# Reordering the picking, the last loads and the last values of each layer in a four-layer decode kernel

## The chip, the cores and the metric

One core of a Trainium2 chip runs the whole program. The metric is the device time of one execution in microseconds (us), as the median of several runs. All runs quoted were in the same (fast) state: the executions of one kernel lie within 0.3% of their median. The span of a profile is the time from its first to its last instruction; over all runs it is 1.7 to 3.6 us shorter than the run's time.

In profiles, PE is the engine for matrix products (PEld its loading of weights), DVE the one for vectors, ACT the one for scalar functions, POOL a general one, and SP issues the loads (its queue is SPq). PSUM is the memory that takes PE's results. The granted clock is the share of its full clock that a throttle leaves PE. K9 is K of pair 9, and so on.

## The reference, cut to what matters

Four attention layers with one query token each; layers 0 and 2 use one set of weights and caches (A), layers 1 and 3 the other (B).

```python
# per layer; D = 640, 32 heads, 8192 keys, head size 192, all bf16
q = layernorm(x) @ wq                         # wq: 640 x 6144
p = softmax(q . k_cache * 192**-0.5)          # k_cache: 32 x 8192 x 192
o = p . v_cache                               # v_cache: 32 x 8192 x 192
x = x + o.reshape(6144) @ wo                  # wo: 6144 x 640
```

Every byte of K and V is used once per layer, so the program mostly streams 848 MB from memory.

## The kernel before

A *pair* is two heads; a layer has 16. Buffers live in a pool of 8 slots of 24 KB per partition; half a pair's K or V (3072 KB) fills one slot. All big loads leave one queue (SP) in the fixed order of a list `plan`. A load stands there until the slots it goes into are free, and every load behind it stands too. `KEPT` holds K of pair 0 from layer 0 to layer 2 and V of pairs 14 and 15 from layer 1 to layer 3, so layer 2 works with four slots.

```python
KEPT = {0: {("k", 0)}, 1: {("v", 14), ("v", 15)}}

# a step list gives the order on the engines; "plan" the order of loads (cut)
steps.append(("m", l, p, 0))              # q*K, first half: DVE product, PE sum
if late is not None:
    steps.append(("e", l, late))          # picking of the pair before
steps.append(("m", l, p, 1))              # q*K, second half
if p == NPAIR - 1:
    steps.append(("v", l, p - 1))
steps.append(("s", l, p))                 # softmax
...
if p == NPAIR - 1:
    steps += [("e", l, p - 1), ("wc", l, 2), ("v", l, p), ("e", l, p)]
...
both(("wo", l, 2), ("wol", l))            # wol: wo's rows of the last pair

def products(p, u):                       # "m": frees the K half when PE is done
    for c in range(4):
        DV.op(k3[.., part c] = kin[.., part c] * q_sb)     # 128 x 3072, in place
    for each group of R columns:
        PE.op(S += ident . k3[.., group])                  # 24 matmuls

def gather(p):                            # "e": the picking
    for i in range(VK):                   # VK = 8
        DV.op(acc (+)= O[:, i*DH:(i+1)*DH] * pick[:, i])   # reads PSUM
    PE.op(TB = half . acc); AC.op(orow = TB / sum)
```

`values` ("v") multiplies V by the probabilities with 8 keys per group, so its result in PSUM has 8 blocks per head of which the picking keeps the diagonal. `columns` ("wc") turns the row of outputs into columns for the product with wo.

## Time and profile before

| | before |
|---|---|
| time, median of the first 3 runs | 2018.94 us (2017.25 to 2019.47) |
| span of the profile | 2015.6 us |
| bytes read | 848.36 MB |
| rate in ten quiet stretches of 110 to 420 us | 430 to 434 GB/s |
| 848.36 MB at 432 GB/s | 1964 us |
| so time lost to less than full transfer | 2015.6 - 1963.8 = 51.8 us |

The first lines are from the profile's page of the kernel before: busy time by engine, then granted TensorE clock and memory rate in 40 slices of about 50 us, then the engines' shares of the chain that ended last (the work followed back from the last instruction, at each step to what released it).

```profile
span 2015.6 us, 13729 instructions
PE 1278.0 (63%) x8246; PEld 146.2 (7%) x3074; DVE 1210.3 (60%) x1395; ACT 139.5 (7%) x461; POOL 4.4 (0%) x22
...
PEclk9787787888688788788877877877787877778777
GB/s 418 429 432 418 427 437 410 436 436 424 436 430 436 414 433 427 402 428 436 428 311 435 427 430 434 428 381 432 433 421 429 435 427 433 436 427 434 434 432 295
DMA packets 25773, 849.24 MB, mean 421 GB/s; under 512 B 3056, under 2 KB 3056, under 8 KB 3696
...
DMA 56%; DVE 24%; PE 18%; ACT 1%; issue 1%; SPq 0%
```

No engine is full, and the rate is flat but for a few slices (311, 381, 402 and the last). The Trainium skill, "DMA: Bandwidth & Descriptors", Anatomy of one DMA, gives the moving part of a transfer as bytes over 436e9 per second, for DMAs that the GpSimd engine issues; the 432 GB/s of this trace, whose loads SP issues, agree within 1%. Only time in which the queue runs dry, and the tail after the last byte, can be saved. The windows view shows five such stretches; three smaller ones, near 174, 325 and 679 us, are not printed here. Its columns are: the stretch in us, its length, busy time and instructions of each engine, granted clock, DMA share, GB/s.

```profile
core 0: us, PE busy (x) PEld busy (x) DVE busy (x) ACT busy (x) POOL busy (x), PEclk, DMA share, GB/s
832.00:838.00 6.00, 3.75 (x28) 0.40 (x12) 1.28 (x4) 1.31 (x5) 0.00 (x0) 0.96 0.48 163
...
1022.00:1028.00 6.00, 3.64 (x79) 3.63 (x80) 2.13 (x6) 0.27 (x1) 0.00 (x0) 0.64 0.05 18
...
1044.00:1048.00 4.00, 4.00 (x22) 0.09 (x3) 2.27 (x3) 0.00 (x0) 0.00 (x0) 1.00 0.04 14
1352.00:1358.00 6.00, 6.00 (x23) 0.10 (x1) 5.49 (x4) 0.00 (x0) 0.00 (x0) 0.77 0.16 70
...
2003.00:2015.60 12.60, 5.65 (x118) 4.83 (x106) 3.57 (x10) 0.27 (x1) 0.00 (x0) 0.64 0.01 0
```

Why the queue was dry at 832 us, the timeline shows. First the SP queue of before (start, length, engine, line, operation; each line is the issue of a load), then DVE and PE at the same place.

```profile
809.38 0.33 SPq L369 DMA_DIRECT2D pool<-in_B_wo_dram  x1
834.88 0.33 SPq L356 DMA_DIRECT2D pool<-in_B_k_cache_dram  x1
...
1005.26 28.58 SPq L363 DMA_DIRECT2D pool<-in_A_wq_dram  x3
1048.06 0.34 SPq L356 DMA_DIRECT2D pool<-in_A_v_cache_dram  x1
...
1333.20 5.77 SPq L358 DMA_DIRECT2D pool<-in_A_k_cache_dram  x2
1357.40 0.80 SPq L358 DMA_DIRECT2D pool<-in_A_v_cache_dram  x2
```

```profile
814.21 6.77 DVE L530 TENSOR_TENSOR pool<-pool,q_sb 128x3072 bf16<-128x3072 bf16 x4 [8.71 <-DMA pool<-in_B_k_cache_dram]
...
821.21 0.42 DVE L616 TENSOR_SCALAR acc<-OY,small 128x192 f32<-128x192 f32 x1
821.67 3.13 DVE L617 SCALAR_TENSOR_TENSOR acc<-OY,small,acc 128x192 f32<-128x192 f32 x7
824.72 6.76 DVE L530 TENSOR_TENSOR pool<-pool,q_sb 128x3072 bf16<-128x3072 bf16 x4
```

```profile
826.92 7.88 PE L58 MATMUL S<-pool,ident 128*128 128x512 bf16 x23
```

K10 is issued at 834.88, 25 us after the load before it, because it goes into the slots of K9. K9 lands at 814.2, but its second half is multiplied only after the 3.7 us of picking, and PE is done with it at 834.8. From 1333.2 the two halves of K10 are issued in layer 2, the second by 1339, and then nothing for 18 us, until 1357.4: V10's first half waits for the slot of K10's first half, and the other half stands behind it.

### The profile page before, as it was taken

The numbers are of one execution on the slowest core, as the hardware profiler recorded it, in microseconds if no ns is written. First come the engines' busy times: TensorE is split into PE (matmuls) and PEld (weight loads), VectorE is DVE, ScalarE is ACT, GpSimd is POOL, SyncE is SP. The second block draws the span as 40 slices with busy tenths as digits, with TensorE's granted clock in tenths as the row PEclk, the third lists the DMA queues.
The fourth block names the chain that finished last, engine by engine and source line by source line (L and its number), as shares of the span: only waits on it lengthen the run. The fifth ranks groups of instructions, "written<-read, shape, count | busy, mean of one in ns | idle before, by whom it ended". The sixth has DMA issues, their size and how long they took to land.

```text
span 2015.6 us, 13729 instructions
## 1 busy us (share of the span) xinstructions
PE 1278.0 (63%) x8246; PEld 146.2 (7%) x3074; DVE 1210.3 (60%) x1395; ACT 139.5 (7%) x461; POOL 4.4 (0%) x22
## 2 busy tenths in 40 slices
PE   3566566566557656566765675675766766666666
PEld 0001001000100100100010010010001001001001
DVE  3566565577356657567744675664764764765765
ACT  0000000000000000000010000000000100000000
POOL 0000000000000000000000000000000000000000
PEclk9787787888688788788877877877787877778777
DMA  9999999999999999999979999999999999999996
GB/s 418 429 432 418 427 437 410 436 436 424 436 430 436 414 433 427 402 428 436 428 311 435 427 430 434 428 381 432 433 421 429 435 427 433 436 427 434 434 432 295
DMA packets 25773, 849.24 MB, mean 421 GB/s; under 512 B 3056, under 2 KB 3056, under 8 KB 3696
## 3 DMA queue, kind: packets, MB, share of 16 engines
q1 hardware_dynamic: 25568, 848.38, 98.0%
q8 instruction: 44, 0.72, 0.1%
q14 instruction: 17, 0.14, 0.0%
q10 hardware_dynamic: 144, 0.00, 0.0%
HBM read 848.36 MB, written 0.00 MB: 421 GB/s over the span
## 4 chain that ended last, share of the span: by engine, by line
DMA 56%; DVE 24%; PE 18%; ACT 1%; issue 1%; SPq 0%
DMA pool<-in_A_k_cache_dram 27%; DMA pool<-in_B_k_cache_dram 27%; DVE pool L530 17%; PE S L58 11%; DVE acc L617 4%; PE OY L58 3%; PE OY L590 2%; DMA pool<-in_B_wq_dram 1%; DMA pool<-in_A_v_cache_dram 1%; PE S L543 1%; ACT p_sb L567 1%; PE OY L501 1%; DVE s_sb L552 1%; DVE acc L616 1%; PE TB L628 0%
## 5 line engine op out<-in xcount | busy, mean ns | idle before, releaser
L530 DVE TENSOR_TENSOR pool<-pool,q_sb 128x3072 bf16<-128x3072 bf16 x512 | 864.3, 1753 | 547.1 <-DMA pool<-in_A_k_cache_dram 279.3
L58 PE MATMUL S<-pool,ident 128*128 128x512 bf16 x2944 | 825.9, 440 | 21.4 <-DVE pool L530 20.9
L543 PE MATMUL S<-pool,ident 128*128 128x512 bf16 x128 | 66.4, 518 | 367.7 <-DVE pool L530 367.5
L58 PE MATMUL OY<-pool,p_sb 128*16 128x512 bf16 x2048 | 202.2, 479 | 0.0
L617 DVE SCALAR_TENSOR_TENSOR acc<-OY,small,acc 128x192 f32<-128x192 f32 x448 | 187.2, 418 | 15.7
L590 PE MATMUL OY<-pool,p_sb 128*16 128x512 bf16 x1024 | 124.8, 475 | 101.5 <-ACT p_sb L567 63.3
L552 DVE TENSOR_REDUCE s_sb<-S 128x64 f32<-128x512 f32 x128 | 88.2, 689 | 78.0 <-PE S L58 78.0
L628 PE MATMUL TB<-acc,small 128*1 128x192 f32 x240 | 56.4, 363 | 120.2 <-DVE acc L617 120.2
L639 ACT ACTIVATE rows<-TB,small 1x192 bf16<-1x192 f32 x120 | 43.2, 405 | 1044.2 <-PE TB L628 1044.2
L567 ACT ACTIVATE p_sb<-s_sb,small 64x128 bf16<-64x128 f32 x128 | 55.7, 435 | 155.8 <-DVE small L561 155.0
L489 ACT ACTIVATE q_sb<-QM 128x192 bf16<-128x192 f32 x60 | 19.9, 331 | 529.3 <-PE QM L483 529.3
L612 DVE RECIPROCAL small<-TB 1x2 f32<-1x2 f32 x64 | 11.2, 175 | 72.5 <-PE TB L599 36.4
L628 PEld LDWEIGHTS TB<-acc,small 128*1 128x1 f32 x240 | 16.1, 86 | 479.9 <-DVE acc L617 467.7
L590 PEld LDWEIGHTS OY<-pool,p_sb 128*16 128x16 bf16 x1024 | 30.1, 104 | 269.1 <-issue 176.1
L543 PEld LDWEIGHTS S<-pool,ident 128*128 128x128 bf16 x128 | 12.9, 101 | 502.7 <-DVE pool L530 495.0
L557 PE MATMUL QM<-ident,m_bf 128*64 128x64 bf16 x128 | 14.1, 216 | 54.4 <-DVE m_bf L554 53.8
L501 PE MATMUL OY<-oT,pool 128*128 128x1 bf16 x900 | 38.1, 178 | 2.2 <-ACT oT L515 2.2
L501 PEld LDWEIGHTS OY<-oT,pool 128*128 128x128 bf16 x900 | 37.0, 131 | 2.9 <-ACT oT L515 2.9
L561 DVE TENSOR_REDUCE small<-QM 128x1 f32<-128x64 f32 x64 | 14.4, 224 | 34.2 <-PE QM L557 34.2
L483 PEld LDWEIGHTS QM<-rows,one_b 1*64 1x64 bf16 x120 | 6.2, 100 | 384.5 <-issue 377.7
L616 DVE TENSOR_SCALAR acc<-OY,small 128x192 f32<-128x192 f32 x64 | 26.7, 417 | 1.9
L567 ACT ACTIVATION_READ_ACCUMULATOR p_sb<-s_sb,small 64x1 f32 x128 | 23.3, 182 | 0.0
(59 smaller groups left out, 179.8 us busy)
## 6 DMA issues: line engine op xcount, KB each, us to landing
pool<-in_B_k_cache_dram SPq DMA_DIRECT2D x30, 6144.0 KB, 35.9
pool<-in_A_v_cache_dram SPq DMA_DIRECT2D x28, 6144.0 KB, 24.7
pool<-in_B_v_cache_dram SPq DMA_DIRECT2D x28, 6144.0 KB, 29.5
pool<-in_A_k_cache_dram SPq DMA_DIRECT2D x16, 6144.0 KB, 32.0
pool<-in_A_k_cache_dram SPq DMA_DIRECT2D x30, 3072.0 KB, 19.2
pool<-in_A_v_cache_dram SPq DMA_DIRECT2D x8, 3072.0 KB, 17.1
pool<-in_A_wo_dram SPq DMA_DIRECT2D x6, 2400.0 KB, 19.6
pool<-in_B_v_cache_dram SPq DMA_DIRECT2D x4, 3072.0 KB, 33.3
```

The lines of the kernel that those rows point to most:

```text
L58: return t.add_instruction(mybir.InstMatmult(name=t.bass.get_next_instruction_name(), engine=mybir.EngineType.PE, ins=[t.lower_ap(rhs), t. ...
L489: lambda a: a.activation(q_sb[i][:], QM[:, 0:DH], ACT.Copy), e, last["q"][i], bank=QMu)
L501: e = PE.op(lambda t, i=i, c=c, f=y_first[0], fin=end and i == k - 1: t.matmul(YB[:, c:c + 1], lhsT=t3[:, i, c:D:DC], rhs=o[:, i:i + 1], s ...
L530: e = DV.op(lambda v, d0=d0: v.tensor_tensor(k3[:, :, d0:d0 + QD], kin[:, :, d0:d0 + QD], q_sb[qi][:, d0:d0 + QD].unsqueeze(1).broadcast_t ...
L543: t.matmul(S[:, :], lhsT=ident[:], rhs=k3[:, :, d0:d0 + R], start=True, stop=fin) if d0 == 0 else
L552: lambda v, u=u: v.tensor_reduce(s[:, u * JU:(u + 1) * JU], SP_[u][:].rearrange("p (j r) -> p j r", r=R), AX.X, ALU.add), ev_S[p, u], last ...
L567: ev_p[p] = AC.op(lambda a, h=h, r=r: a.activation(p_sb[par][r, :, h], s[r, :], ACT.Exp, bias=negm[par][r, 0:1], accum_out=l_col[par][r, h ...
L590: t.matmul(o, lhsT=x, rhs=y, start=f, stop=fin) if c == 0 else
L616: v.tensor_scalar(acc[:], O[:, 0:DH], pick[:, 0:1], None, ALU.mult) if i == 0 else
L617: v.scalar_tensor_tensor(out=acc[:], in0=O[:, i * DH:(i + 1) * DH], scalar=pick[:, i:i + 1], in1=acc[:], op0=ALU.mult, op1=ALU.add)), e if ...
L628: e = PE.op(lambda t, h=h: t.matmul(TB[96:97, C_O + h * DH:C_O + (h + 1) * DH], lhsT=half[:, h:h + 1], rhs=acc[:], start=True, stop=True), ...
L639: last["TO"] = last["row_written"] = AC.op(lambda a, h=h: a.activation(orow[:, o0 + h * DH:o0 + (h + 1) * DH], TB[96:97, C_O + h * DH:C_O ...
```

## The change

It reorders. No byte and no product is dropped, except six of eight picks per layer end.

1. The picking of pair p-1 comes behind both products of pair p.
2. In a layer's last pair, V14's matmuls come between the two products of pair 15; the last part of wo is loaded before V15 and multiplied between (layers 1 and 3: also behind) V15's halves; the last pair takes 2 keys per group, so 2 picks instead of 8.
3. wol goes into the buffer of the q rows, which is free once "wc" is done. With that, wq of layers 2 and 3 can be split 2/2/1 rows instead of 1/2/2.
4. Layer 2's first loads: K1's first half, V0, K1's second half.
5. Where V is loaded in halves, the half whose slot is free earlier goes first (V10 of layer 2).

```diff
-                if late is not None:
-                    steps.append(("e", l, late))
-                    late = None
+                if p == NPAIR - 1:
+                    steps.append(("v", l, p - 1))
                 steps.append(("m", l, p, 1))
...
+                elif p > 0 and p % PAIRS_W > 0 or p > 2 * PAIRS_W:
+                    steps.append(("e", l, p - 1))
                 steps.append(("s", l, p))
...
+                        if l == 2 and p == 1:
+                            i = plan.index(("k", l, 1, 0))
+                            plan[i - 2:i + 1] = [("k", l, 1, 0)] + plan[i - 2:i]
...
-            both(("wo", l, 2), ("wol", l))
+            plan.insert(-2, ("wo", l, 2))
+            steps += [("wc", l, 2), ("v", l, p, 0), ("wo", l, 2), ("v", l, p, 1)]
+            if NB[l]:
+                both(("wob", l))
+            steps.append(("e", l, p))
+            both(("wol", l))
...
+                if n[2] < NPAIR - 1 and not whole(*n[:3]) and max(map(released, before[n])) > max(map(released, before[m])):
+                    plan[i:i + 2] = [m, n]
+                    turn[n[1:3]] = (1, 0)
...
-    Q_PARTS = [[(0, 2), (2, 2), (4, 1)] if l < 2 else [(0, 1), (1, 2), (3, 2)] for l in range(NL)]
+    Q_PARTS = [(0, 2), (2, 2), (4, 1)]
...
-                    wol_rows(l), w["wo"][r0:r0 + PD].rearrange("(p i) n -> p (i n)", p=P)),
+                    rows[:], w["wo"][r0:r0 + PD].rearrange("(p i) n -> p (i n)", p=P)),
...
+                k = 2 if p == NPAIR - 1 else VK
...
-                for i in range(VK):
+                for i in range(2 if end else VK):
```

More of the change, by code (lines that the diff above doesn't have):

```diff
@@ L87, in build @@
     QW = H * DH
-    Q_PARTS = [[(0, 2), (2, 2), (4, 1)] if l < 2 else [(0, 1), (1, 2), (3, 2)] for l in range(NL)]
+    Q_PARTS = [(0, 2), (2, 2), (4, 1)]
     OI = PD // P
-    NB = 3
+    NB = [0, 5, 0, 5]
     G = 4
@@ L238, in build @@
                     steps.append(("wq", l, 1))
-                if late is not None:
-                    steps.append(("e", l, late))
-                    late = None
+                if p == NPAIR - 1:
+                    steps.append(("v", l, p - 1))
                 steps.append(("m", l, p, 1))
@@ L245, in build @@
                 if p == NPAIR - 1:
-                    steps.append(("v", l, p - 1))
+                    steps.append(("e", l, p - 1))
+                elif p > 0 and p % PAIRS_W > 0 or p > 2 * PAIRS_W:
+                    steps.append(("e", l, p - 1))
                 steps.append(("s", l, p))
@@ L249, in build @@
                     both(("wq", l, 1), ("wq", l, 2))
-                if p == NPAIR - 2:
-                    continue
-                vs_ = [p] if p < NPAIR - 1 else [p - 1, p]
-                for i in vs_:
-                    if first_load("v", l, i) == (l, i):
-                        plan += [("v", l, i, u) for u in range(2)]
-                if p == NPAIR - 1:
-                    steps += [("e", l, p - 1), ("wc", l, 2), ("v", l, p), ("e", l, p)]
-                else:
+                if p < NPAIR - 2:
+                    if first_load("v", l, p) == (l, p):
+                        plan += [("v", l, p, u) for u in range(2)]
+                        if l == 2 and p == 1:
+                            i = plan.index(("k", l, 1, 0))
+                            plan[i - 2:i + 1] = [("k", l, 1, 0)] + plan[i - 2:i]
                     steps.append(("v", l, p))
@@ L263, in build @@
                         both(("wo", l, b))
-                    else:
-                        late = p
-            both(("wo", l, 2), ("wol", l))
-        plan.append(("wob", NL - 1))
+            for i in (p - 1, p):
+                if first_load("v", l, i) == (l, i):
+                    plan += [("v", l, i, u) for u in range(2)]
+            plan.insert(-2, ("wo", l, 2))
[4 more added lines that the diff above has]
+            both(("wol", l))
         at = {n: i for i, n in enumerate(steps)}
@@ L275, in released @@
                     l, p = l + 2, ORDER[l + 2]["pairs"].index(pair(l, p))
-                return at[("v", l, p) if n[0] == "v" else ("m", l, p, n[3])]
-            return at[n]
+                return at[("v", l, p, 1) if n[0] == "v" and p == NPAIR - 1 else ("v", l, p) if n[0] == "v" else ("m", l, p, n[3])]
+            return at[("wob", n[1]) if n[0] == "wo" and n[2] == 2 and NB[n[1]] else n]
         place, before, holder = {}, {}, [None] * NSLOT
@@ L284, in allot @@
                 ns = [("wq", n[1], g) for g in range(3)]
-            elif n[0] == "v" or n[0] == "k" and whole(*n[:3]):
+            elif n[0] == "v" and (n[2] < NPAIR - 1 or n[1] == 1) or n[0] == "k" and whole(*n[:3]):
                 ns = [n[:3] + (u,) for u in range(2)]
@@ L301, in build @@
         for n in plan:
-            if n[0] == "wol" and n[1] + 1 < NL:
-                m = ("wq", n[1] + 1, 0)
-                allot(m)
-                before[n] = before[("wq", n[1] + 1, 2)] if n[1] == 0 else before[m]
+            if n[0] == "wol":
+                before[n] = [("wc", n[1], 2)]
             elif n[0] == "wob":
@@ L309, in build @@
                 allot(n)
+        turn = {}
+        for i, n in list(enumerate(plan)):
+            if n[0] == "v" and n[3] == 0:
+                m = n[:3] + (1,)
+                turn[n[1:3]] = (0, 1)
+                if n[2] < NPAIR - 1 and not whole(*n[:3]) and max(map(released, before[n])) > max(map(released, before[m])):
+                    plan[i:i + 2] = [m, n]
+                    turn[n[1:3]] = (1, 0)
         freed, landed = {}, {}
@@ L314, in wq_rows @@
         def wq_rows(l, g):
-            c0, k = Q_PARTS[l][g]
+            c0, k = Q_PARTS[g]
             if l < 2:
@@ L320, in wq_rows @@
             return slot[place[("wq", l, g)]][:, 0:k * QC].rearrange("p (c n) -> p c n", c=k)
-        def wol_rows(l):
-            if l + 1 == NL:
-                i = place[("wol", l)] * TS
-            else:
-                i = place[("wq", l + 1, 0)] * TS + (DC * QW if l == 0 else QC)
-            return pool[:, i:i + OI * D]
         def transfer(n):
@@ L344, in transfer @@
                 return SP.op(lambda s: s.dma_start(
-                    slot[place[("wo", l, 2)]][:, (NW - NB) * D:NW * D],
-                    w["wo"][r0:r0 + PAIRS_W * PD].rearrange("(p i) n -> p (i n)", p=P)[:, (NW - NB) * D:]),
+                    slot[place[("wo", l, 2)]][:, (NW - NB[l]) * D:NW * D],
+                    w["wo"][r0:r0 + PAIRS_W * PD].rearrange("(p i) n -> p (i n)", p=P)[:, (NW - NB[l]) * D:]),
                     sem=semOB, inc=16)
@@ L361, in transfer @@
             elif n[0] == "wq":
-                c0, k = Q_PARTS[l][n[2]]
+                c0, k = Q_PARTS[n[2]]
                 f = lambda s: s.dma_start(
@@ L367, in transfer @@
                 r0 = o["wo"][n[2]] * PD
-                k = NW - NB if n == ("wo", NL - 1, 2) else NW
+                k = NW - NB[l] if n[2] == 2 else NW
                 f = lambda s: s.dma_start(
@@ L456, in q_rows @@
                 n = ("wq", l, g)
-                c0, k = Q_PARTS[l][g]
+                c0, k = Q_PARTS[g]
                 t3 = wq_rows(l, g)[:, :, ORDER[l]["q1"] * PD if l < 2 else 0:]
@@ L491, in layer, with project @@
             y_first = [True]
-            def project(n, rows, o, ev_o):
-                t3 = rows.rearrange("p (i n) -> p i n", n=D)
+            def project(n, w, o, ev_o):
+                t3 = w.rearrange("p (i n) -> p i n", n=D)
                 k = t3.shape[1]
-                end = n == ("wob", l) or n == ("wol", l) and l + 1 < NL
                 PE.wait(ev_o, need(n), last["YB"])
@@ L500, in project @@
                     for c in range(DC):
-                        e = PE.op(lambda t, i=i, c=c, f=y_first[0], fin=end and i == k - 1: t.matmul(
+                        e = PE.op(lambda t, i=i, c=c, f=y_first[0], fin=n[0] == "wol" and i == k - 1: t.matmul(
                             YB[:, c:c + 1], lhsT=t3[:, i, c:D:DC], rhs=o[:, i:i + 1], start=f, stop=fin,
@@ L504, in project @@
                         y_first[0] = False
-                freed[n] = e
+                if n[0] == "wo" and (n[2] < 2 or NB[l] == 0):
+                    freed[n] = e
                 return e
@@ L513, in columns @@
                                                       start=True, stop=True), signal=(i == k - 1), bank=TBu)
-                last["orow"] = e
+                last["orow"] = freed[n] = e
                 last["TT"] = AC.op(lambda a: a.activation(oT[:, 0:k], TB[:, 0:k], ACT.Copy),
@@ L570, in softmax, with values @@
                 last["s"][par] = last["negm"][par] = ev_p[p]
-            def values(p):
+            def values(p, us=(0, 1)):
                 par = (l * NPAIR + p) % 2
                 nl, np_ = first_load("v", l, p)
-                i0 = place[("v", nl, np_, 0)] * TS
-                t = pool[:, i0:i0 + 2 * TS]
+                k = 2 if p == NPAIR - 1 else VK
+                N = min(512, k * DH)
                 PE.wait(ev_p[p], last["O"])
-                rounds = J // VK // G
-                for r in range(rounds):
-                    PE.wait(need(("v", nl, np_, r * 2 // rounds)))
-                    for c in range(3):
+                rounds = J // k // G
+                for r in range(us[0] * rounds // 2, (us[-1] + 1) * rounds // 2):
+                    u, i = divmod(r, rounds // 2)
+                    u = turn[nl, np_][u]
+                    PE.wait(need(("v", nl, np_, u)))
+                    t = slot[place[("v", nl, np_, u)]]
+                    for c in range(k * DH // N):
                         for g in range(G):
-                            j = (r * G + g) * VK
-                            o, x, y = (O[32 * g:32 * g + 2 * VK, c * 512:(c + 1) * 512],
-                                       p_sb[par][:, j:j + VK, :].rearrange("p j h -> p (j h)"),
-                                       t[:, j * DH + c * 512:j * DH + (c + 1) * 512])
+                            j = (i * G + g) * k
+                            o, x, y = (O[32 * g:32 * g + 2 * k, c * N:(c + 1) * N],
+                                       p_sb[par][:, u * JU + j:u * JU + j + k, :].rearrange("p j h -> p (j h)"),
+                                       t[:, j * DH + c * N:j * DH + (c + 1) * N])
                             f, fin = r == 0, r == rounds - 1
@@ L591, in values @@
                                 matmul_held(t, o, x, y, f, fin, 32, 32 * g)),
-                                signal=(fin and c == 2 and g == G - 1), bank=Ou)
+                                signal=(fin and c == k * DH // N - 1 and g == G - 1), bank=Ou)
+                if 1 not in us:
+                    return
                 ev_O[p] = last["p"][par] = e
@@ L649, in layer @@
                 elif n[0] == "v":
-                    values(n[2])
+                    values(n[2], n[3:] or (0, 1))
                 elif n[0] == "e":
@@ L659, in layer @@
                 elif n[0] == "wo":
-                    k = NW - NB if n == ("wo", NL - 1, 2) else NW
+                    k = NW - NB[l] if n[2] == 2 else NW
                     last["oT"] = project(n, slot[place[n]][:, 0:k * D], oT[:, 0:k], last["oTw"])
+                elif n[0] == "wob":
+                    last["oT"] = freed[("wo", l, 2)] = project(
+                        n, slot[place[("wo", l, 2)]][:, (NW - NB[l]) * D:NW * D], oT[:, NW - NB[l]:NW], last["oTw"])
                 else:
                     last["TT"] = last["TTn"]
-                    last["oTl"] = ev_y = project(n, wol_rows(l), oTl, last["TTn"])
-                    if l + 1 == NL:
-                        ev_y = project(("wob", l), slot[place[("wo", l, 2)]][:, (NW - NB) * D:NW * D], oT[:, NW - NB:NW], last["oTw"])
+                    last["oTl"] = ev_y = project(n, rows[:], oTl, last["TTn"])
                 if q_ready and (n[0] == "wq" and l >= 2 or n[0] == "m" and n[3] == 1):
```

## The prediction

> **What bounds it now.** Input bandwidth. The core reads 848 MB; ten undisturbed stretches of 110 to 420 us in the windows view run at 430 to 434 GB/s, DMA share 1.00. 848.36 MB / 0.432 = 1964 us, so about 52 us of the 2015.6 us span lack full transfer. DVE (60%) and PE (63%) have slack in the mean; the chain of waits gives DMA K loads 54%. So I ask only where the DMA queue runs dry (windows of 2 us):
>
> - layer 1 to 2: 1020-1030 and 1044-1048 nearly empty (18 and 14 GB/s in the middle): about 12.5 us lost. Kept V14/V15 hold four slots, K0 two; wq loads wait for the PE's wo work (22.8 us wait of the SP queue) and K0's products.
> - layer 2, pair 10: 1352-1358 at 70 GB/s: 5 us. V10's first half waits for K10's first half; the other half, whose slot is free earlier, stands behind it.
> - pairs 5 and 10 of layers 0/1 (about 174, 325, 679, 832-838): K waits for the previous pair's second product, which waits behind 3.7 us of PSUM picking on DVE: 7 us together.
> - the tail: data ends near 2003, then 12.6 us of compute.
>
> **What the change does.**
> 1. Both products before the picking: the second K half is free 3.5 to 5 us earlier (picking 0.42+3.13 us; it also fills the following 1.5 us wait for S). In steady state nothing, since bandwidth binds. It closes most dips at pairs 5/10. At half clock 24 S matmuls cost about 10 us, over DVE's 6.8, so PE then sets the release: 6 us.
> 2. Swapped V10 halves: 5 us.
> 3. Layer 1 to 2: wo precedes V15, wol takes no slot, wq split 2/2/1 sends more bytes early, K1's first half precedes V0. By my walk through the releases, the 12.5 us hole becomes 0.5-1 us before wq's last part and about 4 us before K1's first half: gain 8 us. After a stall, the queue takes about 2 us to full rate; the Trainium skill, "DMA: Bandwidth & Descriptors", Anatomy of one DMA, gives a fixed cost of about 2.0 us (for another issuing path); this trace agrees: K10 issued at 834.9, full rate near 838.
> 4. Layer 2 to 3: V15 now waits for V14's use instead of K15's; only wo (5.7 us) covers it: lose about 1 us.
> 5. Tail: 2 of 8 picks left (6 x 0.42 = 2.7 us), V14 and picking earlier, most wo matmuls before the last picking. V15's values could start 5 us earlier, but then wait for its second half from the saturated queue: gain 4 to 5 us. V15's PE cost hardly changes: same columns, 64 weight loads for 16.
>
> Sum: 6+5+8-1+4.7 = 23 us, nearly all critical, being queue-empty time or tail. Compute cut in the middle is worth nothing. Bytes are unchanged. Floor: without any dip 1964 + about 10 + the 3 us between span and time is 1977, so over 2% (below 1978.6) is very unlikely.
>
> **Predicted** 1995 us, 8 in 10 within 1987 to 2004; faster by over 2%: 0.04, within 2%: 0.94, slower: 0.02.
>
> **To check.** Mean bandwidth about 426 instead of 421 GB/s; V10 hole gone; the 1020-1048 hole 3-6 us; no dip at pairs 5/10 of layers 0-1; data end to span end 8 us instead of 12.6; accumulating picks 448 to 424.
>
> **What would make it wrong.** wol stands in the in-order queue behind the columns step and could hold up the next layer's loads; V14's matmuls before K15's second product could delay a layer's end; V15 late at layer 2 to 3 could open a larger hole.

## The result, and the profile after

| | before | after |
|---|---|---|
| time, median | 2018.56 us (4 runs) | 1990.81 us (4 runs, 1989.87 to 1991.55) |
| ratio | | 0.9863 (0.9846 to 0.988) |
| span of the profile | 2015.6 us | 1988.6 us |
| mean rate | 421 GB/s | 427 GB/s |

A ratio is the mean time of one kernel's runs over that of the other's of the same rounds, so it is not quite the ratio of the medians. The kernel is 1.4% faster, 28 us.

The page of the kernel after, the lines that answer to those of before:

```profile
span 1988.6 us, 14015 instructions
PE 1287.4 (65%) x8310; PEld 156.0 (8%) x3266; DVE 1196.8 (60%) x1371; ACT 139.4 (7%) x461; POOL 4.4 (0%) x22
...
PEclk9787787777587688787777777878877877878777
GB/s 411 439 428 431 437 430 430 436 430 428 436 429 436 423 431 436 427 434 430 424 393 435 427 428 434 428 430 430 431 403 430 434 431 435 429 438 428 432 436 342
...
DMA 65%; DVE 18%; PE 14%; issue 2%; ACT 1%; SPq 0%
```

Three of the low slices are gone (410, 402, 381), 311 is now 393, and a new one has come (403, the thirtieth slice). The windows view of the kernel after, at the corresponding places and at the new hole:

```profile
828.00:834.00 6.00, 3.94 (x40) 0.59 (x18) 1.10 (x3) 1.70 (x6) 0.00 (x0) 0.61 0.97 419
...
998.00:1002.00 4.00, 3.41 (x28) 1.34 (x21) 2.44 (x6) 1.70 (x6) 0.00 (x0) 1.00 0.75 270
1028.00:1032.00 4.00, 4.00 (x36) 0.27 (x7) 4.00 (x4) 0.00 (x0) 0.00 (x0) 1.00 0.82 277
1332.00:1342.00 10.00, 10.00 (x50) 0.76 (x18) 9.47 (x7) 0.00 (x0) 0.00 (x0) 0.71 1.00 427
1486.00:1492.00 6.00, 6.00 (x53) 0.57 (x11) 2.82 (x8) 0.00 (x0) 0.00 (x0) 0.83 0.62 226
1982.00:1988.60 6.60, 2.77 (x52) 2.57 (x51) 1.05 (x4) 0.27 (x1) 0.00 (x0) 0.50 0.01 0
```

The SP queue of the kernel after, and then DVE and the end of PE's second product, at the places shown of before:

```profile
805.74 0.33 SPq L369 DMA_DIRECT2D pool<-in_B_wo_dram  x1
825.15 0.33 SPq L356 DMA_DIRECT2D pool<-in_B_k_cache_dram  x1
...
1002.40 21.94 SPq L363 DMA_DIRECT2D pool<-in_A_wq_dram  x3
1029.28 0.34 SPq L358 DMA_DIRECT2D pool<-in_A_k_cache_dram  x1
...
1311.48 10.91 SPq L358 DMA_DIRECT2D pool<-in_A_k_cache_dram  x2
1332.75 8.12 SPq L358 DMA_DIRECT2D pool<-in_A_v_cache_dram  x2
```

```profile
810.12 13.44 DVE L530 TENSOR_TENSOR pool<-pool,q_sb 128x3072 bf16<-128x3072 bf16 x8 [10.60 <-DMA pool<-in_B_k_cache_dram]
...
823.80 0.42 DVE L621 TENSOR_SCALAR acc<-OY,small 128x192 f32<-128x192 f32 x1
824.26 3.14 DVE L622 SCALAR_TENSOR_TENSOR acc<-OY,small,acc 128x192 f32<-128x192 f32 x7
```

```profile
823.62 1.46 PE L58 MATMUL S<-pool,ident 128*128 128x512 bf16 x6 [0.21 <-DVE pool L530]
```

From K9's landing to K10's issue it was 834.9 - 814.2 = 20.7 us and is 825.2 - 810.1 = 15.0 us: eight product instructions in one run of 13.44 us, the picking behind them.

To add this up I use one account for every run. I read the rate in windows of 10 us, count each window as lost by (432 - GB/s)/432 of its length, and sum from the start. The running sum, averaged over a quiet stretch between two stages, gives what was lost up to there; the end is span minus 1963.8 us. The values carry about 0.4 us of noise (two profiles of the kernel after differ by at most 0.3 us in any stage). The last row holds about 2 us in every run that no window shows as lost (the windows add up to 49.6 us before and 22.8 us after, the rows to 51.8 and 24.8); in differences it drops out.

| lost, us | before | after | gain | predicted |
|---|---|---|---|---|
| start | 1.8 | 1.8 | 0 | 0 |
| layers 0 and 1 (dips at pairs 5, 10) | 9.7 | 1.0 | 8.7 | 6 |
| layer 1 to 2 | 14.3 | 5.4 | 8.9 | 8 |
| layer 2, pair 5 | 0.7 | 0.6 | 0.1 | 0 |
| layer 2, V10 | 6.1 | 0.6 | 5.5 | 5 |
| layer 2 to 3 | 1.2 | 3.5 | -2.3 | -1 |
| tail | 18.0 | 12.0 | 6.0 | 4.7 |
| sum | 51.8 | 24.8 | 27.0 | 23 |

This account says where time went, not yet why. For that I ran experiments.

### The profile page after: what moved, and what is told of

The parts are those of the page before. It is cut to its first block, busy times and chain, and to the rows that moved or that the text cites. A ratio compares the mean times of both kernels' runs of the same rounds, so it can differ in the third digit from the quotient of the medians.

```text
span 1988.6 us, 14015 instructions
## 1 busy us (share of the span) xinstructions
PE 1287.4 (65%) x8310; PEld 156.0 (8%) x3266; DVE 1196.8 (60%) x1371; ACT 139.4 (7%) x461; POOL 4.4 (0%) x22
## 4 chain that ended last, share of the span: by engine, by line
DMA 65%; DVE 18%; PE 14%; issue 2%; ACT 1%; SPq 0%
DMA pool<-in_B_k_cache_dram 28%; DMA pool<-in_A_k_cache_dram 19%; DVE pool L530 14%; DMA pool<-in_A_v_cache_dram 14%; PE S L58 5%; PE OY L58 4%; DMA pool<-in_B_v_cache_dram 4%; PE OY L593 3%; DVE acc L622 2%; DMA pool<-in_A_wq_dram 1%; DVE s_sb L552 1%; ACT p_sb L567 1%; PE OY L500 0%; PE S L543 0%; DVE acc L621 0%
## 5 line engine op out<-in xcount | busy, mean ns | idle before, releaser
L58 PE MATMUL S<-pool,ident 128*128 128x512 bf16 x2944 | 791.0, 426 | 19.2 <-DVE pool L530 17.3
L543 PE MATMUL S<-pool,ident 128*128 128x512 bf16 x128 | 62.6, 489 | 316.4 <-DVE pool L530 316.4
L593 PE MATMUL OY<-pool,p_sb 128*16 128x512 bf16 (+1 forms) x1216 | 156.2, 541 | 128.2 <-DMA pool<-in_A_v_cache_dram 59.4
L58 PE MATMUL OY<-pool,p_sb 128*16 128x512 bf16 x1920 | 219.1, 547 | 0.0
L622 DVE SCALAR_TENSOR_TENSOR acc<-OY,small,acc 128x192 f32<-128x192 f32 x424 | 177.2, 418 | 14.9
L552 DVE TENSOR_REDUCE s_sb<-S 128x64 f32<-128x512 f32 x128 | 83.4, 683 | 14.7 <-PE S L58 14.6
L593 PEld LDWEIGHTS OY<-pool,p_sb 128*16 128x16 bf16 (+1 forms) x1216 | 37.9, 114 | 332.6 <-issue 225.7
L557 PE MATMUL QM<-ident,m_bf 128*64 128x64 bf16 x128 | 15.1, 233 | 40.6 <-DVE m_bf L554 39.7
## 6 DMA issues: line engine op xcount, KB each, us to landing
pool<-in_A_wo_dram SPq DMA_DIRECT2D x6, 2400.0 KB, 20.7
```

The costliest lines, as they stand in the source:

```text
L58: return t.add_instruction(mybir.InstMatmult(name=t.bass.get_next_instruction_name(), engine=mybir.EngineType.PE, ins=[t.lower_ap(rhs), t. ...
L543: t.matmul(S[:, :], lhsT=ident[:], rhs=k3[:, :, d0:d0 + R], start=True, stop=fin) if d0 == 0 else
L552: lambda v, u=u: v.tensor_reduce(s[:, u * JU:(u + 1) * JU], SP_[u][:].rearrange("p (j r) -> p j r", r=R), AX.X, ALU.add), ev_S[p, u], last ...
L593: t.matmul(o, lhsT=x, rhs=y, start=f, stop=fin) if c == 0 else
L622: v.scalar_tensor_tensor(out=acc[:], in0=O[:, i * DH:(i + 1) * DH], scalar=pick[:, i:i + 1], in1=acc[:], op0=ALU.mult, op1=ALU.add)), e if ...
```

## The experiments

Eleven runs were timed in five rounds, those of one call on one chip. All outputs are right. The table has the medians, ratios to the kernel before, and the lost time by stage of each run's profile (the start and pair 5 of layer 2, together 2 to 3.3 us, are only in the last column).

| run | median us | ratio to before | layers 0, 1 | 1 to 2 | V10 | 2 to 3 | tail | sum with the rest |
|---|---|---|---|---|---|---|---|---|
| before | 2018.56 | 1 | 9.7 | 14.3 | 6.1 | 1.2 | 18.0 | 51.8 |
| after | 1990.81 | 0.9863 | 1.0 | 5.4 | 0.6 | 3.5 | 12.0 | 24.8 |
| after_again | 1991.99 | 0.9871 | 1.3 | 5.7 | 0.4 | 3.7 | 11.8 | 25.3 |
| a1_pick_between | 2002.99 | 0.993 | 9.3 | 6.6 | 0.6 | 4.0 | 11.6 | 34.6 |
| a2_v10_in_order | 1996.58 | 0.9894 | 1.3 | 5.7 | 5.1 | 2.9 | 12.0 | 29.4 |
| a3_eight_keys | 1996.1 | 0.9895 | 1.0 | 8.8 | 0.2 | 5.1 | 15.1 | 33.6 |
| a4_v14_late_l2 | 1988.18 | 0.9855 | 0.4 | 5.8 | 0.2 | 0.5 | 12.4 | 22.2 |
| b1_wq_122 | 1992.74 | 0.9871 | 0.8 | 7.6 | 1.2 | 3.6 | 11.9 | 27.5 |
| b2_k1_after_v0 | 1996.77 | 0.9894 | 1.3 | 11.0 | 2.1 | 3.9 | 11.7 | 32.6 |
| b3_wo_after_v15 | 1987.79 | 0.9849 | 0.6 | 5.1 | 0.6 | 2.1 | 11.0 | 21.3 |
| b4_only_picks | 2005.68 | 0.994 | 0.8 | 13.5 | 6.1 | 0.5 | 15.8 | 39.1 |
| c1_v15_first_v14_late | 1987.48 | 0.9848 | 1.2 | 5.4 | 0.4 | 0.4 | 12.2 | 22.0 |
| d1_only_wol_rows | 2018.75 | 1.0006 | 10.3 | 14.7 | 6.1 | 1.4 | 17.6 | 52.2 |

### The kernel after once more: after_again

> The kernel after, unchanged, as a reference on the same chip: 1990 to 1992 us, ratio to before 0.985 to 0.988.

The kernel after, unchanged, beside the last runs: 1991.99 us against 1990.81, and each stage within 0.3 us of its first profile. So differences of about 1 us between runs of different calls mean nothing here. Only c1 and d1 ran with it; the a runs and the b runs were on two other chips. Where a difference of medians is small, the ratios to before are the fairer comparison.

### The picking: a1 (undone) and b4 (done alone)

```diff
 a1, on the kernel after (shortened)
+                if p < NPAIR - 1 and (p > 0 and p % PAIRS_W > 0 or p > 2 * PAIRS_W):
+                    steps.append(("e", l, p - 1))     # behind m 0
-                elif p > 0 and p % PAIRS_W > 0 or p > 2 * PAIRS_W:
-                    steps.append(("e", l, p - 1))     # behind m 1
 b4, on the kernel before (shortened)
-                if late is not None: ... steps.append(("e", l, late))    # behind m 0
+                if late is not None: ... steps.append(("e", l, late))    # behind m 1
```

> Kernel after, with the picking of a pair put back between the next pair's two products (last pairs of a layer untouched). Theory (the second K half is freed late, so the queue runs dry before pairs 5 and 10): 6 to 9 us slower than after, about 1998 us, with the low windows back near pairs 5 and 10 of layers 0 and 1 and no change in the tail. Rival (those dips were closed by the other parts of the change): within 2 us of after.

> Kernel before, with only the picking moved behind both products. Theory (parts add): the four dips at pairs 5 and 10 of layers 0 and 1 go, about 8.5 us, and the layer ends, the V10 hole and the tail stay: about 2009 us. Rival (in before, something else holds those loads as well): under 4 us gained.

Undone, 8.3 us are lost again in layers 0 and 1, and in time 12 us (2002.99 against 1990.81; its five runs spread from 2000.31 to 2004.69, and the profiled one was the fastest, with 9.8 us more lost in all). That is more than the 6 to 9 us I expected; what the slower runs lost beyond that has no trace and stays open. Done alone, the loss there falls from 9.7 to 0.8 us. So the picking's place explains this stage whole, from both sides. In b4, K10 of layer 1 is issued at 825.09 us, in the kernel after at 825.15; the SP queue of b4:

```profile
825.09 0.33 SPq L356 DMA_DIRECT2D pool<-in_B_k_cache_dram  x1
```

But b4 gains 13.3 us in time (2018.98 to 2005.68, the medians), not the 8.5 I expected: the tail loses 2.2 us less, and the two layer changes 0.8 and 0.7 us less. In the tail the picking of pair 13 now stands where DVE waited for PE's sums: from K14's first product to K15's it takes 19.3 us instead of 20.9. That is 1.6 us of the 2.2; the rest is not traced. The rivals of both runs (under 2 us, under 4 us) have fallen.

### V10's halves: a2

```diff
-                if n[2] < NPAIR - 1 and not whole(*n[:3]) and max(...) > max(...):
+                if n[2] < NPAIR - 1 and not whole(*n[:3]) and False and max(...) > max(...):
```

> Kernel after, with V10's halves of layer 2 loaded first half first again. Theory: one hole of 5 to 6 us comes back in layer 2 at pair 10 and nothing else changes, about 1996 us. Rival (the later free K slots of the new order already cover it): under 2 us.

Measured: 5.8 us slower, and one stage grows, V10 from 0.6 to 5.1 us. The hole is back, here in the windows view of a2:

```profile
1334.00:1340.00 6.00, 6.00 (x25) 0.10 (x1) 5.47 (x4) 0.00 (x0) 0.00 (x0) 0.87 0.30 126
```

The kernel after moved 427 GB/s over 1332 to 1342 us.

### Keys per group: a3

```diff
-                k = 2 if p == NPAIR - 1 else VK
+                k = VK
-                for i in range(2 if end else VK):
+                for i in range(VK):
```

> Kernel after, with 8 keys per group and 8 picks in the last pairs. 6 more picks of 0.42 us in each of the four layer ends. Theory: they count at the program's end (2.5 us) and at layer 1 to 2, where the next loads wait for the chain (up to 2.5 us), and not at 0 to 1 and 2 to 3: 3 to 5 us slower, about 1995 us. Rival A: all four ends count, 10 us. Rival B: hidden everywhere, 0 us.

Measured: 5.3 us slower by the medians (its four runs lie between 1994.48 and 1999.41), and 8.8 us by its profile, which was of the slowest run. By stages: 3.1 us in the tail, 3.4 us at layer 1 to 2, 1.6 us at layer 2 to 3, nothing at 0 to 1. I had expected nothing at 2 to 3. The end at 0 to 1 costs nothing, as expected; the size was just over my range of 3 to 5 us by the medians, and well over it in the profile. The profile of a3 shows what the six picks cost in the tail (compare the single accumulating pick of the kernel after, 0.42 us at 1982.50):

```profile
1988.56 3.13 DVE L622 SCALAR_TENSOR_TENSOR acc<-OY,small,acc 128x192 f32<-128x192 f32 x7
```

That is 2.7 us of the tail's 3.1. The edit also changes the shape of V15's matmuls, a rival I had not named; in the tail it costs nothing, for from the start of V15's second half to PE's next step it takes 2.67 us in a3 and 2.66 us in the kernel after. At 1 to 2 the two were not told apart.

### V14 in layer 2: a4

```diff
-                if p == NPAIR - 1:
+                if p == NPAIR - 1 and l != 2:
                     steps.append(("v", l, p - 1))
                 steps.append(("m", l, p, 1))
+                if p == NPAIR - 1 and l == 2:
+                    steps.append(("v", l, p - 1))
```

> Kernel after, with V14's matmuls behind K15's second product again in layer 2 only, so that V15's first half takes K15's slot. Theory (V15 waits for V14's landing and use, only wo is queued meanwhile): the hole at 1486 to 1492 us closes and the kernel gains 2 to 3 us, about 1988.5 us. Rival (the hole only moves into layer 3, whose slots now come in another order): within 1 us of after.

The new hole of the kernel after, in its timeline: wo is issued at 1477.20, then the PE stands 7 us for V14's landing, with K15's second product behind it in its order, and V15's halves are issued when V14 has been used.

```profile
1477.20 0.33 SPq L369 DMA_DIRECT2D pool<-in_A_wo_dram  x1
1484.22 0.60 PE L593 MATMUL OY<-pool,p_sb 128*16 128x512 bf16 x4 [7.05 <-DMA pool<-in_A_v_cache_dram]
...
1488.89 0.80 SPq L358 DMA_DIRECT2D pool<-in_A_v_cache_dram  x2
```

In a4 K15's second product goes first, V15's first half takes its slot at 1482.78, and the stretch is full (windows view of a4, then its SP queue):

```profile
1484.00:1492.00 8.00, 3.59 (x54) 0.87 (x22) 4.36 (x11) 0.00 (x0) 0.00 (x0) 0.97 1.00 426
```

```profile
1482.78 4.86 SPq L360 DMA_DIRECT2D pool<-in_A_v_cache_dram  x2
```

Measured: 2.6 us faster than after by the medians, 1.6 us by the ratios, whose intervals overlap (0.9841 to 0.9868 and 0.9846 to 0.988). What is clear is the stage: 2 to 3 falls from 3.5 to 0.5 us, and the sum from 24.8 to 22.2. The theory held there; the rival (the hole only moves) did not.

### The place of wo: b3, and both together: c1

```diff
 b3
-            plan.insert(-2, ("wo", l, 2))
-            steps += [("wc", l, 2), ("v", l, p, 0), ("wo", l, 2), ("v", l, p, 1)]
+            plan.append(("wo", l, 2))
+            steps += [("wc", l, 2), ("v", l, p, 0), ("v", l, p, 1), ("wo", l, 2)]
 c1: b3 and a4 together
```

> Kernel after, with the last wo loaded and used after both halves of V15 instead of around them, all else as in after. Theory from the gaps of after's trace (998 to 1002 us: V15's second half waits for K15's second product; 1486 to 1492 us: only wo covers V14): V15 as the earlier load covers both better and V15's second half lands earlier, so this is faster than after, by 2 to 5 us, 1986 to 1989; the place of wo was then no gain of the change. Rival (wo around V15 is what shrinks the layer ends and the tail): 2 us or more slower than after.

> Kernel after with the last wo behind both halves of V15 (run b3) and V14's matmuls behind K15's second product in layer 2 (run a4). Theory: what is still lost at layer 2 to 3 in b3 (2.1 us) falls to about 0.5 us, the rest as in b3: 1985 to 1987 us, 4 to 6 us faster than after, faster than every other version. Rival (both do the same thing): no faster than b3, 1988 us.

b3 is 3.0 us faster than after by the medians (2.8 us by the ratios, whose intervals overlap; c1, below, which has this edit too, was run beside the kernel after). The stages that fall beyond the noise are 2 to 3 (by 1.4 us) and the tail (by 1.0 us); 1 to 2 falls by 0.3 us only. So wo around V15 was no gain of this change. The wait for V15's second half in the tail shows it, here in the kernel after and then in b3 (the PE waits 3.40 us and then 1.12 us, and starts at 1978.90 and at 1972.66):

```profile
1978.90 2.73 PE L593 MATMUL OY<-pool,p_sb 128*4 128x384 bf16 x32 [3.40 <-DMA pool<-in_B_v_cache_dram]
```

```profile
1972.66 2.73 PE L593 MATMUL OY<-pool,p_sb 128*4 128x384 bf16 x32 [1.12 <-DMA pool<-in_B_v_cache_dram]
```

The end itself moves less than these 6 us, because in b3 the PE then waits 0.9 us for wo and does all 75 of its matmuls there (3.19 us); in the kernel after 50 of them were done before.

c1 has the hole at 2 to 3 closed as expected (0.4 us instead of b3's 2.1), but it is no faster than b3 in time: 1987.48 against 1987.79, intervals of the ratios 0.9834 to 0.9861 and 0.9835 to 0.9862. Its tail lost 1.2 us more than b3's, and small differences in the other stages took the rest. Whether the closed hole is worth anything on top of b3 stays open. Against the kernel after, c1 is 4.5 us faster (1987.05 to 1987.57 against 1990.80 to 1993.66 us; ratios 0.9848 and 0.9871), 0.2%. b3 and a4 are within 1 us of it.

### The parts of layer 1 to 2: b1, b2, d1

```diff
 b1
-    Q_PARTS = [(0, 2), (2, 2), (4, 1)]
+    Q_PARTS = [[(0, 2), (2, 2), (4, 1)] if l < 2 else [(0, 1), (1, 2), (3, 2)] for l in range(NL)]
 b2
-                        if l == 2 and p == 1:
-                            i = plan.index(("k", l, 1, 0))
-                            plan[i - 2:i + 1] = [("k", l, 1, 0)] + plan[i - 2:i]
 d1, on the kernel before: wol loaded into rows[:], released by ("wc", l, 2)
```

> Kernel after, with wq of layers 2 and 3 split 1/2/2 as before instead of 2/2/1. My prediction credited the split with part of the gain at layer 1 to 2. A new walk with after's times: the queue then dries some 3.4 us earlier before wq's second part (gap about 1 us), but a larger last part covers the wait for K1's first half (2 us gap goes). Theory: within 1.5 us of after, 1989.5 to 1992. Rival (the prediction's reading): 3 us slower.

> Kernel after, with layer 2's first loads in the old order, V0 before both halves of K1. Theory: after wq's last part nothing can be issued until K0's second product is done, so the hole at 1028 to 1032 us grows to some 9 us: about 7 us slower than after, near 1998. Rival (only slots and the wo position matter): within 2 us of after.

> Kernel before, with only wol moved to the q rows' buffer and so behind the columns step. Theory: wol and wq's first part at layer 1 to 2 are issued about 10 us later, just when the queue would run dry: within 2 us of before, the 1020 us hole only starts earlier. Rival (wol's slot space was what held back wq): 3 us or more faster. The risk that my prediction named: 3 us or more slower.

b2 is 6.0 us slower, with 5.6 us more lost at 1 to 2 (and 1.5 us more at V10). Its SP queue shows nothing issued from about 1023 us, when the last of three wq parts is out, until V0 at 1035:

```profile
1001.91 21.56 SPq L360 DMA_DIRECT2D pool<-in_A_wq_dram  x3
1035.46 0.34 SPq L353 DMA_DIRECT2D pool<-in_A_v_cache_dram  x1
```

In the kernel after, K1's first half fills that stretch from 1029.28 (shown above). The order of these loads is the largest single part of this stage.

b1 lost 2.2 us more at 1 to 2 in its profile, but its time is 1992.74 against 1990.81 and 1991.99 of the kernel after, with ratios that overlap (0.9871 against 0.9863 and 0.9871). It fits neither my new theory nor its rival well; the split 2/2/1 is worth 0 to 3 us.

d1 is no different from before (1.0006, 0.9992 to 1.0019). Moving wol alone is worth nothing, and its new wait behind "wc" costs nothing: wq's first part is issued at about 1016 instead of 1005 us, but the queue ran dry only past 1020 us anyway. The SP queue of d1:

```profile
1015.98 18.36 SPq L357 DMA_DIRECT2D pool<-in_A_wq_dram  x3
```

In the change the move is what makes room for two rows of wq in the first part: 2 x 5760 + 1920 elements of wol are more than a slot's 12288.

## Why the prediction was right or wrong

The time, 1990.81 us, lies in the range of 1987 to 2004, and 4 us below the middle. Point by point:

- **What bounds it: right.** The bytes stayed, the quiet rate stayed at 432 GB/s (431 in layer 3 of b3 and c1), and 27.0 us of span came out of 51.8 us of lost time. DVE lost 13.5 us of busy time and PE gained 9.4 us without that showing in the quiet stretches.
- **Term 1, the picking, 6 us: right in kind, too small.** Measured 8.7 us in the account, 8.3 undone, 8.9 done alone in the same stage. What was mis-sized is the loss there was to win back: I put the four dips at 7 us together, and the account, read between the quiet stretches around each, has 1.9, 1.8, 2.3 and 3.7 us, together 9.7. Of 7 I forecast 6; of 9.7 came 8.7. The dips differ with the granted clock of the 8 us that end 0.5 us before K's issue. In the three runs with the picking between the products (before, d1, a1) the loss of one dip is 1.7 to 2.0 us at a clock of 1.00 (seven dips), 2.3 to 3.0 us at 0.79 (three) and 3.7 and 4.1 us at 0.62 (two). So my 7 us was about what four dips at full clock lose. And I had thought that at half clock PE would hold K up after the change. That half clock did not come: in the ten runs with the picking behind both products the clock at these 40 places was 0.94 to 1.00, where five of the 12 with the picking between were at 0.62 to 0.79. At K10 of layer 1, 23 matmuls of the second product took 7.88 us in before (clock 0.50 over 826 to 832 us); in the kernel after it was done 1.5 us after DVE's last chunk (clock 1.00 over 820 to 825 us). a1 and b4 move nothing but the picking, so its place is what changes the clock here. The Trainium skill, "TensorE: Matmul & The Clock Gate", What's actually happening, says that the default is throttled and that activity releases it; that fits, for the picking's break in PE's work lay between the products before and lies behind them now.
- **Term 2, V10, 5 us: right.** 5.5 us, and 4.5 to 5.8 undone.
- **Term 3, layer 1 to 2, 8 us: right in sum, partly by luck; wrong in some parts.** 8.9 us, and 5.4 us stay lost where I said 4.5 to 5. I credited wo before V15, wol's place, wq's split and K1's order alike. The order of K1 and V0 is worth 5.6 us (b2). wo before V15 is worth nothing (b3 loses 0.3 us less without it). wol's place is worth nothing alone (d1). Two keys per group shortened this stage by 3.4 us (a3), which I had not counted here at all. The parts overlap, so they add to more than 8.9. That the queue takes about 2 us to full rate after a stall holds: in the trace's records of before, the first piece of K10 (issued at 834.88) moves 0.95 us later and all 16 DMA engines after 2.0 us, and for V0 at 1048.06 and V10 at 1357.40 all 16 move after 1.5 to 2.0 us. The Trainium skill, "DMA: Bandwidth & Descriptors", Anatomy of one DMA, has a fixed cost of about 2.0 us for DMAs issued by GpSimd, setup and completion together; that is another span than the one measured here, so the like number confirms nothing.
- **Term 4, layer 2 to 3, -1 us: right in kind, too small.** It is -2.3 us. From V14's first matmul to V15's issue took 4.7 us (1484.22 to 1488.89), at a granted clock of 0.50 (1482 to 1488 us) after the PE's 7 us wait; with the 2 us or so until a new load runs at full rate, wo's 5.7 us did not cover that. a4, which lets V15 go without waiting for V14's matmuls, shows that this order is the cause.
- **Term 5, the tail, 4.7 us: right, somewhat small.** 6.0 us: 3.1 of them come with the two keys per group (a3; 2.7 are the six picks), 2.2 us already come with the moved picking (b4). wo around V15 works against it (b3).
- **The risks I named.** wol behind "wc" holding up loads did not happen (d1). V14's matmuls before K15's second product did harm at 2 to 3, the only place where a run took it back (a4); V15 coming late there is the same hole. A gain of over 2% was out of reach, as the floor in the prediction said.
- **The signs I named in the profile: nearly all as said.** Mean rate 427 GB/s (said 426), 6.6 us without data at the end (said 8), 424 accumulating picks on the page (said 424), 5.4 us lost at layer 1 to 2 (said 3 to 6).

## What to carry to other kernels

When bandwidth binds, count only the time in which the queue is empty, by stage, and ask for each empty stretch which release its next load waits for; an account of lost time by stage against the quiet rate makes every experiment readable. In an in-order queue, put first the load whose space comes free first, and put work that frees space (both products here) before work that frees none (the picking). A layer end that ran well as a whole can still hold a part that costs: two parts of this change, undone together, made it 4.5 us faster (c1).

## What the Trainium skill lacked or had wrong

- "TensorE: Matmul & The Clock Gate", What's actually happening: it names the half rate as the state after at least one idle window of about 3.4 us. Here the granted clock of before was 1.00 over 820 to 824 us, 0.91 over 824 to 826 and 0.50 over 826 to 832, though the matmuls' only breaks since 816 us were of 2.1 us (822.7 to 824.9) and 0.9 us, with 0.8 us of work between; no break was 3.4 us long. Of the 12 places with the picking between the products (before, a1, d1), the seven where the first break was of 0.9 to 1.3 us kept a clock of 1.00, and the five where it was of 1.5 to 2.1 us fell to a mean of 0.62 to 0.79; no run varied the break alone, so this is no threshold. The page gives no length for breaks short of a window (it speaks elsewhere of short idles between groups of matmuls, without one), and it does not say that moving another engine's work can close them.
- "DMA: Bandwidth & Descriptors", Issuing engines are not separate DMA queues: it says that DMAs of different engines interleave. A load of 1.2 KB issued on the ACT queue at 0.73 us, beside loads of 7680 and 6144 KB issued on SP at 0.74 and 1.18 us, took 21.5 us to land, as long as the 7680 KB (21.3 us). Its 128 pieces of 10 bytes start one by one from 4.6 to 21.7 us, while the large loads run. A small load beside large ones of another queue can thus take all of their time; the page gives no number for that.
- The same page, Anatomy of one DMA, has its fixed cost for DMAs issued by GpSimd only. The kernel's last store of 1.2 KB on the SP queue, with nothing else under way, took 2.6 us to land in before and 2.8 us in after.
- "Perfetto Trace Analysis", What "DMA-bound" means: it lacks the case of this kernel, a queue that is bound by bandwidth but runs dry in a few places because no buffer is free (elsewhere the page names too few buffers for gaps that repeat), and the account of lost time by stage against the kernel's own quiet rate that showed it (51.8 us lost before, 24.8 us after).
